# TensorE's instruction order laid out matmul by matmul in a fused attention and gated-MLP kernel

## The chip, the cores and the metric

The kernel runs on one core of one Trainium2 chip. Its time is in device microseconds (us) per execution. Engines are named PE (TensorE, matrix multiply), ACT (ScalarE), DVE (VectorE), POOL (GpSimd) and SP (SyncE, which here only starts DMA transfers). PE writes into PSUM; ACT and DVE read it out. Each engine works through its own queue in order, and an instruction waits for semaphores that others set.

## The reference

A layer normalisation of `x` (2048 x 640) feeds two branches. Branch A is attention in four segments of 512 rows with 32 heads of 20, causal inside a segment, joined by a memory of the earlier segments that is read through the feature map `phi`. Branch B is a gated MLP.

```python
xn = layernorm(x)
for s in range(4):                        # segments of 512 rows
    p = softmax(qs @ ks.T * scale + mask)
    a_dot = p @ vs
    a_mem = (phi(qs) @ M) / (phi(qs) @ z + 1e-6)
    o = g * a_mem + (1 - g) * a_dot       # g = sigmoid(beta), per head
    M, z = M + phi(ks).T @ vs, z + phi(ks).sum()
s = concat(o) @ wo                        # phi(t) = t + 1 if t > 0 else exp(t)
h = sigmoid(xn @ w_gate) * (xn @ w_up)
return x + s * silu(h @ w_down)
```

## The kernel before

Everything is bf16 with f32 sums. The order of all five engines is written out by hand: a Python planner calls functions that emit instructions, and the order of the calls is the order in each queue.

**Score batches and weighting passes.** A segment has 20 slots: four pairs of head groups, five units each (`UNITS`). In each slot `scores` (L471) emits one batch of 4 or 8 matmuls on four row strips of the array at once into the one PSUM tile `Sps`, ACT's exponential of 128 x 2048 (L482), and POOL's causal mask (L485). `weigh` (L489) multiplies the masked result by the values with 8 to 24 matmuls of 21 columns (L502) into the tile `Aps`, of which there is one; DVE then normalises it (L508 to L511).

**Dense groups.** A dense group is a chain of matmuls into one of three rotating PSUM buffers (`ps_d`), then an evacuation. `gate` (L386) and `up` (L394): five of 512 columns, then Tanh on ACT, or the product on DVE, which also needs gate's Tanh. `down` (L405): twelve of 320 columns, Tanh on ACT, product on DVE. `v_tile` (L313): five of 320, cast on ACT. `k_chunk`, `q_chunk` (L249, L274): five of 512, cast on DVE. `o_proj` (L450): five of 320, DVE. `m_update` (L343) and `mem_read` (L363) write and read the memory.

**The planner.** Gate, up and down groups wait in a list, `bulk`, with their cost in us. All else stands in a heap, `tasks`, with a due time in slots (`at`); the factor `R` is 20/24 slots, and `later` puts a step some of these units after the current time. Per slot the main loop (L628) emits `scores`, then fills 45% of the slot's budget, then emits the weighting passes of the slot before, then fills the other 55%. A fill runs the tasks that are due and whole bulk groups as long as half a group's cost is owed. So batches and passes always stand between groups. In the last segment three down groups are kept back for the end (`keep`).

**Features.** `phi` (L324) turns keys and queries into features: two DVE passes, Exp on ACT 0.5 units later, a maximum on DVE 0.5 units after that, and for keys a DMA transpose into `pkt` 0.7 units after that (L339), which `m_update` needs. The calls have fixed due times. The tile of keys (`k5`) has one buffer, so the next segment's keys wait for the transposes. Outgoing transfers of keys and queries (`stage_out`) read the same tiles that `phi` then overwrites.

**Startup.** Before the first slot: warm-up matmuls, normalisation of four row tiles (`ln_stats`: statistics on DVE, rstd on POOL; `ln_norm`: scaling on DVE L222, transposes on PE L229, copy on ACT), then all v, k, q groups of segment 0 and six gate and up groups.

Of the kernel before, what the change touches and what calls it, by code (L numbers as in the profile page):

```python
# [52 lines left out]
R = NSLOT / 24  # L53


@with_exitstack
def kernel(
# [37 lines left out]
    tasks = []  # L95
    count = [0]
    clock = [0.0]
# [5 lines left out]
    def later(lag, fn, *a):  # L103
        at(clock[0] + lag * R, 0.0, fn, *a)

# [143 lines left out]
    def k_chunk(n, c):  # L249
        s = st[n]  # L250
        if c == 0:
            s["k5"] = stg.tile([P, DC, L], BF, name="k5")
            s["kabs"] = stg.tile([P, DC], F32, name="kabs")
        ps = ps_d.tile([P, L], F32, name="psk", tag="d")
        for k in range(DC):
            nc.tensor.matmul(ps[:], lhsT=W["k"][:, k, c * P:(c + 1) * P], rhs=s["xnT"][:, k, :],  # L256
                             start=(k == 0), stop=(k == DC - 1))
        evacuate(n, s["k5"][:, c, :], ps[:])
        nc.vector.tensor_reduce(out=s["kabs"][:, c:c + 1], in_=s["k5"][:, c, :], axis=AX.X, op=ALU.max,  # L259
                                apply_absolute_value=True)  # L260
        if c in (2, 4) and n:
            later(0.9, stage_out, n, c // 4, Ks, KT, "k5")
        if c == DC - 1:
            s["IK"] = stg.tile([P, DC, H], BF, name="IK")
            nc.vector.tensor_tensor(s["IK"][:], nInd[:], s["kabs"][:].unsqueeze(2).to_broadcast([P, DC, H]),
                                    op=ALU.mult)

    def stage_out(n, half, src, dst, name):
        a, b = ((0, 3), (3, 5))[half]
        nc.sync.dma_start(src[n % 2][a * P:b * P, :].rearrange("(c p) n -> p c n", p=P), st[n][name][:, a:b, :])  # L270
        if n:
            later(1.0, relay, n, half, src, dst)

    def q_chunk(n, c):  # L274
        s = st[n]
        if c == 0:
            s["q5"] = stg.tile([P, DC, L], BF, name="q5")
            s["aq"] = stg.tile([P, DC, L], BF, name="aq")
        ps = ps_d.tile([P, L], F32, name="psq", tag="d")
        for k in range(DC):  # L280
            nc.tensor.matmul(ps[:], lhsT=W["q"][:, k, c * P:(c + 1) * P], rhs=s["xnT"][:, k, :],  # L281
                             start=(k == 0), stop=(k == DC - 1))
        evacuate(n, s["q5"][:, c, :], ps[:])
        nc.vector.tensor_scalar(s["aq"][:, c, :].bitcast(U16), s["q5"][:, c, :].bitcast(U16), 0x7FFF, None,
                                op0=ALU.bitwise_and)
        if c in (2, 4) and n:
            later(0.9, stage_out, n, c // 4, Qs, QT, "q5")

    def q_bound(n):
        s = st[n]  # L290
        ps = ps_d.tile([H, L], F32, name="cps", tag="d")
        for c in range(DC):
            nc.tensor.matmul(ps[:], lhsT=s["IK"][:, c, :], rhs=s["aq"][:, c, :],  # L293
                             start=(c == 0), stop=(c == DC - 1))
        cb = stg.tile([H, L], BF, name="cb")
        nc.scalar.copy(cb[:], ps[:])

        if n:
            later(0.8, c_out, n, cb)
        else:  # L300
            c_out(n, cb)

# [10 lines left out]
    def v_tile(n, j, half):  # L313
        s = st[n]
        ps = ps_d.tile([P, HB], F32, name="psv", tag="d")
        for k in range(DC):
            nc.tensor.matmul(ps[:], lhsT=s["xnT"][:, k, j * P:(j + 1) * P],  # L317
                             rhs=W["v"][:, k, half * HB:(half + 1) * HB],
                             start=(k == 0), stop=(k == DC - 1))
        va = V[4 * (n % 2) + j]  # L320
        nc.scalar.copy(va[:, half * 16:(half + 1) * 16, 0:DH], ps[:].rearrange("p (h e) -> p h e", e=DH))  # L321


    def phi(n, src, c):  # L324
        t = st[n][src][:, c, :]
# [8 lines left out]
        def rest():  # L334
            nc.vector.tensor_tensor(t, t, mn[:], op=ALU.max)
            if src == "k5":
                if c == 0:
                    st[n]["pkt"] = stg.tile([P, 4, D], BF, name="pkt")
                later(0.7, lambda: nc.sync.dma_start_transpose(st[n]["pkt"][:, :, c * P:(c + 1) * P], t))  # L339
        later(0.5, exp)  # L340


    def m_update(n, cs):  # L343
        s = st[n]
        dm = ps_d.tile([P, len(cs), HW * VW], F32, name="dm", tag="d")
        for i, c in enumerate(cs):
            w = (H1[c] - H0[c]) * VW
            for j in range(4):
                nc.tensor.matmul(dm[:, i, 0:w], lhsT=s["pkt"][:, j, c * P:(c + 1) * P],
                                 rhs=V[4 * (n % 2) + j][:, H0[c]:H1[c], :].rearrange("p h e -> p (h e)"),  # L350
                                 start=(j == 0), stop=(j == 3))
        for i, c in enumerate(cs):
# [10 lines left out]
    def mem_read(n, j, b):  # L363
        s = st[n]
        if j == 0 and b == 0:
            s["om"] = opool.tile([P, 4, D], BF, name="om", bufs=1)
        am = ps_d.tile([P, 16, VW], F32, name="am", tag="d")
        parts = [c for c in range(DC) if H0[c] < 16 * b + 16 and H1[c] > 16 * b]
        for i, c in enumerate(parts):
# [11 lines left out]
            am[:, :, 0:DH], rm[:].unsqueeze(2).to_broadcast([P, 16, DH]), op=ALU.mult)  # L381


    def gate(n, f):
# [3 lines left out]
        for k in range(DC):  # L388
            nc.tensor.matmul(gp[:], lhsT=Wg[f // 4][:, k, fo:fo + P], rhs=s["xnT"][:, k, :],  # L389
                             start=(k == 0), stop=(k == DC - 1))  # L390
        s["tg"] = gpool.tile([P, L], BF, name="tg")
        nc.scalar.activation(s["tg"][:], gp[:], ACT.Tanh, scale=0.5)  # L392

    def up(n, f):  # L394
# [3 lines left out]
        for k in range(DC):  # L398
            nc.tensor.matmul(ps[:], lhsT=Wu[f // 4][:, k, fo:fo + P], rhs=s["xnT"][:, k, :],  # L399
                             start=(k == 0), stop=(k == DC - 1))  # L400
        h = gpool.tile([P, L], BF, name="hT", bufs=FC)
        nc.vector.scalar_tensor_tensor(out=h[:], in0=s["tg"][:], scalar=1.0, in1=ps[:], op0=ALU.add, op1=ALU.mult)  # L402
        s.setdefault("hT", []).append(h)

    def down(n, j, half):  # L405
# [5 lines left out]
        for f in range(FC):  # L411
            nc.tensor.matmul(yp[:], lhsT=s["hT"][f][:, j * P:(j + 1) * P], rhs=W["d"][:, f, hs],  # L412
                             start=(f == 0), stop=(f == FC - 1))
        t2 = fpool.tile([P, HB], BF, name="t2")
        nc.scalar.activation(t2[:], yp[:], ACT.Tanh, scale=0.25)  # L415
        nc.vector.scalar_tensor_tensor(out=s[f"aa{j}"][:, hs], in0=t2[:], scalar=1.0, in1=yp[:],  # L416
                                       op0=ALU.add, op1=ALU.mult)

# [31 lines left out]
    def o_proj(n, j, half):  # L450
        s = st[n]
        aa, xr = s[f"aa{j}"], s[f"xr{j}"]
# [3 lines left out]
        for c in range(DC):  # L456
            nc.tensor.matmul(sp[:], lhsT=s["oT"][:, j, c, :], rhs=W["o"][:, c, hs],  # L457
                             start=(c == 0), stop=(c == DC - 1))
        nc.vector.scalar_tensor_tensor(out=aa[:, hs], in0=aa[:, hs], scalar=0.25, in1=sp[:],  # L459
# [4 lines left out]
        elif half == 1:  # L464
            (nc.gpsimd if n == NSEG - 1 else nc.vector).tensor_tensor(xr, aa[:], xr, op=ALU.add)
            later(0.9, lambda: nc.sync.dma_start(o2[rows, :], xr))

# [48 lines left out]
    bulk = [(1.09, fn, (0, f)) for f in range(FC) for fn in (gate, up)]  # L516

    def take(k):
        for _, fn, a in bulk[:k]:
            fn(*a)  # L520
# [7 lines left out]
    def startup():  # L528
# [5 lines left out]
        warm(10)  # L534
        ln_stats(0, 1, 0, 1)
        ln_norm(0, 0, 1)
        v_tile(0, 0, 0)
        ln_stats(0, 1, 1, 2)
        ln_norm(0, 1, 0)
        v_tile(0, 1, 0)  # L540
        ln_norm(0, 1, 1)
        v_tile(0, 2, 0)
        for j in range(3):
            v_tile(0, j, 1)
# [3 lines left out]
        for c in range(DC):  # L548
            k_chunk(0, c)
        nc.gpsimd.memset(KT[2][:], 1.0)  # L550
        stage_out(0, 0, Ks, KT, "k5")
        for c in range(DC):
            q_chunk(0, c)
# [7 lines left out]
        v_tile(0, 3, 0)  # L561
        v_tile(0, 3, 1)
        relay(0, 0, Qs, QT)
        q_bound(0)
# [18 lines left out]
    for n in range(NSEG):  # L583
        w = NSLOT * n
        m = n + 1
        if m < NSEG:
# [7 lines left out]
            for c in range(DC):  # L594
                at(w + R * (9.6 + 0.75 * c), 1.08, k_chunk, m, c)
                at(w + R * (13.4 + 0.75 * c), 1.08, q_chunk, m, c)
                at(w + R * (12.6 + 0.8 * c), 0.0, phi, m, "k5", c)
                at(w + R * (18.8 + 0.7 * c), 0.0, phi, m, "q5", c)
# [4 lines left out]
            if n == 0:  # L603
                for c in range(DC):
                    at(R * (2.6 + 0.8 * c), 0.0, phi, 0, "k5", c)
            for i, cs in enumerate(([0, 1, 2], [3, 4])):
                at(w + R * ((8.9 if n else 9.9) + i), 0.6, m_update, n, cs)
        if n >= 1:
# [3 lines left out]
            for i in range(8):  # L612
                at(w + R * (6.6 + i), 0.68, o_proj, n - 1, i // 2, i % 2)
                at(w + R * (3.0 + 0.75 * i), 0.35, mem_read, n, i // 2, i % 2)
# [5 lines left out]
    def run_task():  # L620
        time, _, cost, fn, a = heapq.heappop(tasks)
        clock[0] = max(clock[0], time)
        fn(*a)
        return cost

    owed = 0.0
    due, held = [], []
    for n in range(NSEG):  # L628
        st[n]["od"] = opool.tile([P, 4, D], BF, name="od")
        if n:  # L630
            bulk += [(1.09, fn, (n, f)) for f in range(FC) for fn in (gate, up)]
        bulk += [(1.64, down, (n, j, h)) for j in range(4) for h in range(2)]
        keep = 3 if n == NSEG - 1 else 0
        total = sum(b[0] for b in bulk[:len(bulk) - keep])
        total += sum(t[2] for t in tasks if t[0] < NSLOT * (n + 1))
        budget = total / NSLOT
        for slot in range(NSLOT):
            pair, u = divmod(slot, NU)
            now = NSLOT * n + slot

            def fill(until, share):
                nonlocal owed
                owed += budget * share
                while True:
                    if tasks and tasks[0][0] < until:
                        owed -= run_task()
                        if not (bulk and len(bulk) > keep and owed >= bulk[0][0] / 2):
                            continue
                    if bulk and len(bulk) > keep and owed >= bulk[0][0] / 2:
                        cost, fn, a = bulk.pop(0)  # L650
                        owed -= cost
                        fn(*a)
                    elif not (tasks and tasks[0][0] < until):
                        break

            pt = scores(n, pair, u)
            fill(now + 0.45, 0.45)
            for w in due:
                weigh(*w)
            due, held = held, []  # L660
# [3 lines left out]
            fill(now + 1.0, 0.55)  # L664
        while len(bulk) > keep:
            cost, fn, a = bulk.pop(0)
            owed -= cost
            fn(*a)


    for w in due:
        weigh(*w)
    while tasks:
        run_task()
    n = NSEG - 1
    for j in range(4):
        o_add(n, j, (DC - 1) * P, D)
    for i, (cost, fn, a) in enumerate(bulk):
        if i == len(bulk) - 1:
            o_last(n)  # L680
        fn(*a)
    for j in range(4):
        for h in range(2):
            o_proj(n, j, h)
            while tasks:
                run_task()
# [29 lines left out]
```

## Time and profile before

| | us |
|---|---|
| median of 3 runs | 349.03 (348.88 to 349.73) |
| the profiled execution, its own time | 350.11 |
| its span in the profile | 348.4 |
| PE's matmuls, start of the first score batch to the last matmul | 35.0 to 343.9 |
| segments 0, 1, 2 (first batch to first batch) | 72.8, 82.4, 82.4 |
| busy: PE, ACT, DVE, POOL | 330.7, 229.6, 227.6, 101.6 |

Times in the profile are from the start of the span. "L482" is line 482 of the kernel. In tables of waits a row reads: engine and line that waited, who ended the wait, total us, times, longest. In a timeline a row reads: start, length (of several merged instructions from first start to last end), engine, line, operation, tiles, count, and in brackets the engine's idle time before and who ended it. A matmul's length includes its way through the array, so starts, not lengths, tell the pace.

### The profile page before, as it was taken

To read this page: it belongs to the slowest core of one execution; us is meant where nothing else is said; L and a number is where in the kernel's file an instruction comes from. 1 tells how busy PE (TensorE), PEld (TensorE's weight loads), DVE (VectorE), ACT (ScalarE), POOL (GpSimd) and SP (SyncE) were. 2 spreads that over 40 slices of the span, in tenths; PEclk is the share of its full clock that TensorE was granted. 3 is DMA by queue.
4 is the path that set the end of the run, shared out by engine and by line. 5 is a ranking of instruction groups with operands and counts; after the bars stand their busy time and mean duration, and the time that the engine had idled before them with its cause. 6 is when DMAs were issued, how large, how long until landed. Compare 5 with 4: busy or idle time off the path is not lost.

```text
span 348.4 us, 8338 instructions
## 1 busy us (share of the span) xinstructions
PE 330.7 (95%) x3359; PEld 188.1 (54%) x3402; DVE 227.6 (65%) x581; ACT 229.6 (66%) x248; POOL 101.6 (29%) x135
## 2 busy tenths in 40 slices
PE   6999998997999999999999999999999999999995
PEld 5644445543665456654466446654456555545663
DVE  4252685499566576899655896699756478544355
ACT  2554869667796766557687676646778777767830
POOL 5930323232233233032222331312222232332314
PEclk9899999999999999999999999999999999999999
DMA  7964746565810851046840361123640140220032
GB/s 224 360 223 159 174 120 168 154 189 143 186 43 6 109 96 34 24 134 90 186 94 2 65 103 43 41 93 96 164 92 3 21 116 19 68 86 2 0 62 75
DMA packets 56581, 35.40 MB, mean 102 GB/s; under 512 B 31200, under 2 KB 56544, under 8 KB 56544
## 3 DMA queue, kind: packets, MB, share of 16 engines
q1 hardware_dynamic: 53024, 30.79, 36.2%
q10 hardware_dynamic: 3520, 4.10, 3.8%
q8 instruction: 26, 0.43, 0.5%
q14 instruction: 11, 0.09, 0.1%
HBM read 19.80 MB, written 8.00 MB: 80 GB/s over the span
## 4 chain that ended last, share of the span: by engine, by line
PE 69%; DVE 17%; issue 4%; ACT 4%; DMA 4%; POOL 1%; SPq 0%; DVEq 0%; ACTq 0%; POOLq 0%
PE yp L412 14%; PE up L399 12%; PE gp L389 12%; PE Aps L502 7%; PE Sps L477 6%; PE psq L281 5%; PE psv L317 5%; PE sp L457 5%; ACT pt L482 3%; DMA pkt<-k 2%; PE psk L256 2%; DVE k L247 2%; DVE kabs L259 2%; DVE hT L402 2%; PE cps L293 1%
## 5 line engine op out<-in xcount | busy, mean ns | idle before, releaser
L482 ACT ACTIVATE pt<-Sps 128x2048 bf16<-128x2048 f32 x80 | 150.1, 1876 | 33.2 <-PE Sps L477 32.0
L485 POOL TENSOR_SCALAR_AFFINE_SELECT pt<-pt 128x1024 bf16<-128x1024 bf16 (+1 forms) x80 | 75.9, 949 | 223.7 <-ACT pt L482 223.7
L399 PE MATMUL up<-xnT,Wu 128*128 128x512 bf16 x231 | 59.3, 379 | 1.0 <-DVE aa L459 0.5
L389 PE MATMUL gp<-xnT,Wg 128*128 128x512 bf16 x215 | 57.9, 379 | 1.5 <-issue 0.2
L412 PE MATMUL yp<-Wd,hT 128*128 128x320 bf16 x384 | 57.3, 299 | 0.0
L402 DVE SCALAR_TENSOR_TENSOR hT<-tg,up 128x512 bf16<-128x512 bf16 x48 | 32.8, 683 | 32.0 <-PE up L399 30.3
L502 PEld LDWEIGHTS <-pt 128*128 128x128 bf16 x1280 | 42.8, 96 | 14.3 <-issue 2.3
L502 PE MATMUL Aps<-va,pt 128*128 128x21 bf16 x1280 | 44.6, 173 | 1.1 <-POOL pt L485 0.7
L412 PEld LDWEIGHTS <-hT 128*128 128x128 bf16 x384 | 35.1, 97 | 15.3 <-issue 3.0
L392 ACT ACTIVATE tg<-gp 128x512 bf16<-128x512 f32 x48 | 28.5, 593 | 17.4 <-PE gp L389 17.4
L416 DVE SCALAR_TENSOR_TENSOR aa<-t,yp 128x320 bf16<-128x320 bf16 x32 | 15.6, 487 | 33.5 <-ACT t L415 33.3
L477 PE MATMUL Sps<-QT,KT 21*128 21x128 bf16 (+3 forms) x512 | 31.7, 300 | 4.4 <-ACT pt L482 4.3
L399 PEld LDWEIGHTS <-Wu 128*128 128x128 bf16 x240 | 20.9, 97 | 23.7 <-issue 3.4
L389 PEld LDWEIGHTS <-Wg 128*128 128x128 bf16 x240 | 20.3, 97 | 22.2 <-issue 4.1
L331 ACT ACTIVATE mn<-mn 128x512 bf16<-128x512 bf16 x35 | 22.1, 631 | 13.2 <-DVE mn L327 13.2
L317 PE MATMUL psv<-Wv,xnT 128*128 128x320 bf16 x160 | 27.7, 309 | 0.3 <-DVE hT L402 0.3
L457 PE MATMUL sp<-Wo,oT 128*128 128x320 bf16 x160 | 25.8, 299 | 0.0
L415 ACT ACTIVATE t<-yp 128x320 bf16<-128x320 f32 x32 | 14.0, 437 | 17.1 <-PE yp L412 17.1
L477 PEld LDWEIGHTS <-KT 21*128 21x128 bf16 x512 | 9.5, 92 | 28.7 <-issue 27.4
L256 PE MATMUL psk<-xnT,Wk 128*128 128x512 bf16 x94 | 23.9, 379 | 0.7 <-DVE k L247 0.3
L281 PE MATMUL psq<-xnT,Wq 128*128 128x512 bf16 x97 | 23.8, 380 | 0.5 <-DVE hT L402 0.4
L321 ACT CAST va<-psv 128x320 bf16<-128x320 f32 x32 | 13.7, 431 | 14.6 <-PE psv L317 14.1
(74 smaller groups left out, 330.4 us busy)
## 6 DMA issues: line engine op xcount, KB each, us to landing
KT<-Ks SPq DMA_DIRECT2D x32, 80.0 KB
QT<-Qs SPq DMA_DIRECT2D x32, 80.0 KB
xr<-in_A_x_dram SPq DMA_DIRECT2D x15, 160.0 KB
out_dram<-xr SPq DMA_DIRECT2D x15, 160.0 KB
xt<-in_A_x_dram SPq DMA_DIRECT2D x6, 320.0 KB
Wd<-in_B_w_down_dram ACTq DMA_DIRECT2D x1, 1920.0 KB
Ks<-k SPq DMA_DIRECT2D x4, 384.0 KB
Qs<-q SPq DMA_DIRECT2D x4, 384.0 KB
```

The costliest lines, as they stand in the source:

```text
L256: nc.tensor.matmul(ps[:], lhsT=W["k"][:, k, c * P:(c + 1) * P], rhs=s["xnT"][:, k, :], start=(k == 0), stop=(k == DC - 1))
L281: nc.tensor.matmul(ps[:], lhsT=W["q"][:, k, c * P:(c + 1) * P], rhs=s["xnT"][:, k, :], start=(k == 0), stop=(k == DC - 1))
L317: nc.tensor.matmul(ps[:], lhsT=s["xnT"][:, k, j * P:(j + 1) * P], rhs=W["v"][:, k, half * HB:(half + 1) * HB], start=(k == 0), stop=(k == ...
L389: nc.tensor.matmul(gp[:], lhsT=Wg[f // 4][:, k, fo:fo + P], rhs=s["xnT"][:, k, :], start=(k == 0), stop=(k == DC - 1))
L399: nc.tensor.matmul(ps[:], lhsT=Wu[f // 4][:, k, fo:fo + P], rhs=s["xnT"][:, k, :], start=(k == 0), stop=(k == DC - 1))
L402: nc.vector.scalar_tensor_tensor(out=h[:], in0=s["tg"][:], scalar=1.0, in1=ps[:], op0=ALU.add, op1=ALU.mult)
L412: nc.tensor.matmul(yp[:], lhsT=s["hT"][f][:, j * P:(j + 1) * P], rhs=W["d"][:, f, hs], start=(f == 0), stop=(f == FC - 1))
L457: nc.tensor.matmul(sp[:], lhsT=s["oT"][:, j, c, :], rhs=W["o"][:, c, hs], start=(c == 0), stop=(c == DC - 1))
L477: nc.tensor.matmul(Sps[:, r, c0:c0 + ncol], lhsT=kt[32 * r:32 * r + VW, gi, kb * P:(kb + 1) * P], rhs=qt[32 * r:32 * r + VW, gi, kb * P:L] ...
L482: nc.scalar.activation(pt[:], Sps[:], ACT.Exp, scale=SCALE)
L485: nc.gpsimd.affine_select(out=diag, in_=diag, compare_op=ALU.is_ge, fill=0.0, base=0, pattern=[[0, 4], [0, cnt], [1, P]], channel_multipli ...
L502: nc.tensor.matmul(A[:, qb, r, :], lhsT=pt[:, r, off:off + P], rhs=V[4 * (n % 2) + kb][:, 4 * g + r, :], start=first, stop=True, skip_grou ...
```

## The change

Each function that emits matmuls becomes a generator which hands control back after every matmul with its cost (0.216 us for 512 columns, 0.136 for 320). The planner keeps one unit open (`cur`), takes the next from tasks that are due (`ready`) and otherwise from `bulk`, and moves its position `pos` by cost over budget; weighting passes count as well. Batches and passes are emitted when `pos` reaches the slot's begin and its middle, also inside an open group.

```diff
+    def step(keep):
+        if cur[0] is None:
+            if ready:
+                cur[0] = ready.pop(0)
+            elif len(bulk) > keep:
+                _, fn, a = bulk.pop(0)
+                cur[0] = fn(*a)
+            else:
+                return None
+        cost = next(cur[0], None)
...
+    def advance(target, budget, keep):
...
+            if pos[0] >= target:
+                return
+            cost = step(keep)
+            if cost is None:
+                pos[0] = min(target, tasks[0][0]) if tasks else target
+            else:
+                pos[0] += cost / budget
...
@@ gate; k_chunk, q_chunk, q_bound, v_tile, up, down, o_proj alike
             nc.tensor.matmul(gp[:], lhsT=Wg[f // 4][:, k, fo:fo + P], rhs=s["xnT"][:, k, :],
                              start=(k == 0), stop=(k == DC - 1))
+            if k < DC - 1:
+                yield T512
         s["tg"] = gpool.tile([P, L], BF, name="tg")
         nc.scalar.activation(s["tg"][:], gp[:], ACT.Tanh, scale=0.5)
+        yield T512
...
@@ the main loop
             pt = scores(n, pair, u)
-            fill(now + 0.45, 0.45)
+            advance(now + 0.5, budget, keep)
             for w in due:
                 weigh(*w)
+                pos[0] += weigh_cost(w[2], w[3]) / budget
...
-            fill(now + 1.0, 0.55)
+            advance(now + 1.0, budget, keep)
```

Features go through a queue: at most two are under way, a new one starts at the earliest 0.75 units after the last, and they are pushed when the outgoing transfer has been emitted.

```diff
+    def phi_go():
+        if phis and live[0] < 2 and not held_back[0]:
+            live[0] += 1
+            held_back[0] = True
+            later(0.75, phi_next)
+            phi(*phis.pop(0))
...
@@ phi
-        later(0.5, exp)
+        later(0.8, exp)
@@ stage_out
+            for c in range(a, b):
+                later(1.9 if name == "q5" else 0.7, phi_push, n, name, c)
```

Due times, kept groups, startup and end:

```diff
-                at(w + R * ((8.9 if n else 9.9) + i), 0.6, m_update, n, cs)
+                at(w + R * (10.0 + i), 0.7, m_update, n, cs)
...
-                at(w + R * (3.0 + 0.75 * i), 0.35, mem_read, n, i // 2, i % 2)
+                at(w + R * (4.0 + 0.75 * i), 0.2, mem_read, n, i // 2, i % 2)
...
-        keep = 3 if n == NSEG - 1 else 0
+        keep = 4 if n >= NSEG - 2 else 0
...
         warm(10)
+        ln_norm(0, 0, 1)
         ln_stats(0, 1, 0, 1)
-        ln_norm(0, 0, 1)
...
+    take(1)
     for w in due:
         weigh(*w)
```

The four groups that segment 2 keeps back are down groups; they are the first of segment 3's list. At the end one of the last four down groups comes ahead of the last weighting pass, two behind it, then the last transposes of the attention output (`o_last`), then the fourth. Every matmul, activation and transfer of the old program is in the new one, once.

## The prediction, made before the changed kernel ran

> **What bounds the kernel now.** I read the page first, then the waits, the chain of waits, and the timeline around each wait of the tensor engine (PE).
>
> ```profile
> PE 330.7 (95%) x3359; PEld 188.1 (54%) x3402; DVE 227.6 (65%) x581; ACT 229.6 (66%) x248; POOL 101.6 (29%) x135
> ```
>
> PE is busy for 95% of the span, so only its order, its waits and the two ends can give time. What its work weighs is in the chain of waits, whose pieces are start, length, what:
>
> ```profile
> 29.69 1.08 PE up L399 x5
> ...
> 58.07 7.70 DMA pkt<-k
> ...
> 92.33 1.64 PE yp L412 x12
> ```
>
> One 512-column matmul takes 1.08/5 = 0.216 us, one 320-column matmul 1.64/12 = 0.136. In the same way a weighting matmul (L502) takes 0.025, a memory matmul 0.065, and a score batch 0.41: 0.32 from its first matmul to the next dense one, and about 0.09 more that its first start comes late. From the first batch at 35.02 to the end of the last matmul at 343.85 the program has 615 x 0.216 + 664 x 0.136 + 132 x 0.065 + 1280 x 0.025 + 80 x 0.41 = 296.8 us of work (and 0.2 of transposes). 308.8 passed, so 12.0 us is all that a better order can win there. By segment the loss is 5.9, 1.6, 1.6 and 2.9 us. Going from start to start, I find 9.9 us of it in nineteen gaps of 0.14 to 1.26 us. The waits view (us, times, longest) names who ended the largest:
>
> ```profile
> PE Sps L477 <- ACT pt L482: 4.3, 6, 1.2
> ...
> PE am L371 <- DVE om L379: 0.8, 2, 0.4
> PE Aps L502 <- POOL pt L485: 0.7, 1, 0.7
> ```
>
> The first row is the score batch: one PSUM tile `Sps`, which the exponential (L482) must have read before the next batch may write it. A typical case:
>
> ```profile
> 79.36 1.86 ACT L482 ACTIVATE pt<-Sps 128x2048 bf16<-128x2048 f32 x1
> ...
> 80.07 0.56 PE L502 MATMUL Aps<-va,pt 128*128 128x21 bf16 x16
> ...
> 81.27 0.40 PE L477 MATMUL Sps<-QT,KT 21*128 21x512 bf16 x4 [0.64 <-ACT pt L482]
> ...
> 81.59 1.25 PE L281 MATMUL psq<-xnT,Wq 128*128 128x512 bf16 x5
> ```
>
> The slot before it held one dense group and 16 weighting matmuls, 1.9 us of work; the exponential alone takes 1.86. In start-to-start gaps the seven such waits cost 0.97, 0.68, 1.26, 0.67, 0.38, 0.14 and 0.72 = 4.8 us. They stand after slots with 1.7 to 2.3 us of work, but for the 1.26, where a feature exponential ran ahead on ACT.
>
> **The change, part by part.**
>
> *Even slots.* The new order has the same matmuls. Priced by the same rows, its slots hold 3.3 to 3.5 us of work in segment 0 (before: 1.9 to 4.5), 3.9 to 4.3 in segment 1, 3.6 to 3.9 in segment 2 and 2.9 to 3.2 in segment 3; four down groups of segment 2 go into segment 3, where slots went down to 1.7. An exponential starts 0.5 us after its batch and takes 1.88, so 2.4 us suffice while less than 0.6 to 1.0 us of other ACT work stands ahead of it. I added up ACT's work between exponentials in the new order: in segment 0 it goes up to 4.2 us in one slot, but what spills over, at most 0.8, fits. One batch stays late, by 0.3. Term: -4.8 + 0.3 = -4.5 (bounds -4.8 and -3.0).
>
> *What a cut group does to ACT.* Before, every batch stood between groups, so the evacuation of the group before it was in ACT's queue ahead of the exponential:
>
> ```profile
> 210.00 0.39 PE L477 MATMUL Sps<-QT,KT 21*128 21x512 bf16 x4
> ...
> 210.11 0.43 ACT L321 CAST va<-psv 128x320 bf16<-128x320 f32 x1 [1.58 <-PE psv L317]
> ...
> 210.51 1.88 ACT L482 ACTIVATE pt<-Sps 128x2048 bf16<-128x2048 f32 x1
> ```
>
> Now 64 of the 80 batches cut a group open, 19 of them a gate or a v group. That group's Tanh or cast is issued after the exponential and waits it out, and the third group from there needs its buffer (`ps_d` has three). The worst place, slot 7 of segment 2: the batch cuts a v group after two of five matmuls; then come 3 x 0.136, a memory read 0.2 and a projection group 0.68, so the third group is due 0.32 + 0.41 + 0.20 + 0.68 = 1.6 us after the batch began; its buffer is free after 0.5 + 1.88 + 0.32 (the cast, which overlaps the exponential's end by 0.1) + 0.06 = 2.76. PE waits 1.1 us; DVE's chain behind it does not wait longer. Going through all batches this way, twelve places come out late: 0.46, 0.54, 0.18 in segment 0; 0.80, 0.81, 0.67 in segment 1; 0.18, 0.06, 0.35, 0.14, 1.07 in segment 2; 0.40 and 0.21 (one exponential, I count 0.40) in segment 3: 5.7 us. The same reading of the old order gives 0.2. At three of them PE stood already for DVE beside memory reads (gaps of 0.54, 0.55, 0.69 before), and PE waits once where two things are late; I take 1.5 off: +4.2 (bounds +1.5, if most overlap, and +9.1, if all 19 pay the mean of 0.48).
>
> *The switch itself.* A batch begins 0.10 later than the stream would and the next matmul 0.09 later, 80 times in the old order. The Trainium skill, "TensorEngine Tiling (Array Packing)", Key Properties, says that a change of tiling mode drains TensorE. Read as a warning, it speaks against cutting groups: 64 further drains of 0.19 would be 12 us. But each batch leaves and re-enters the dense stream once in both orders, so I add nothing; the rows cannot show a cut group, so up to 0.05 a batch stays in the range (3 us). A weighting pass amid dense matmuls costs 0.02 at its edges before, and nothing more is added.
>
> *Features.* The Min, Exp and Max passes are as many as before; the queue only spaces them, in ACT and DVE time that the sums above hold. Their steps come 2.0 instead of 1.7 units after each other, so the last `pkt` transpose of segment 0 is issued about 0.25 slot, 0.9 us, nearer to the 1.9 MB load of `Wd`, which stretched the transfer to the 7.70 us in the chain. DVE's cast of `k` waited 2.0 us for it and PE lost 0.5 behind that; everything in DVE's queue waits too, hT and the release of `Aps` first. Term +0.3 (0 to +1.5). Later m_update and mem_read: 0; what needs them is four units on. SP's other issues keep their order but for one or two places.
>
> *Startup.* The second normalisation (L222) moves ahead of the statistics of the next tile:
>
> ```profile
> 5.30:8.70 3.40, 1.67 (x26) 1.33 (x25) 2.15 (x7) 0.69 (x1) 1.48 (x4) 1.00 1.00 303
> 8.70:12.10 3.40, 3.40 (x22) 2.22 (x19) 1.88 (x5) 1.81 (x3) 2.77 (x11) 0.51 1.08 378
> ```
>
> ```profile
> 6.92 0.49 DVE L211 BATCH_NORM_STATS2 bs<-xt 128x6 f32<-128x320 bf16 x1 [1.22 <-DMA xt<-in_A_x_dram]
> ...
> 7.97 0.39 DVE L222 TENSOR_SCALAR xn<-xt,mv,rstd 128x640 bf16<-128x640 bf16 x1
> ...
> 8.42 0.46 PE L229 MATMUL pT<-ident,xn 128*128 128x128 bf16 x5 [1.65 <-DVE xn L222]
> ```
>
> (The first two: stretch, its length, busy PE, PEld, DVE, ACT, POOL, then granted clock, DMA share, GB/s.) Its rstd is ready at 6.40, so it fits DVE's idle 1.22 us: transposes at 6.9 and the first v group at 7.3 instead of 8.7. What is late next is the second pair: x lands at 6.92, statistics and rstd end at 9.1, so the fourth tile's v group starts near 12.0 at the half clock of the second stretch, or near 11.1 at the full clock, instead of 12.46. Term -0.9 (bounds -0.5, -1.4). The Trainium skill, "TensorE: Matmul & The Clock Gate", Part 1, says that an idle window of some 3.4 us halves the clock; the 0.51 after a stretch with 1.67 us of work agrees, and if 2.3 us of work there kept the clock, the term would be the larger.
>
> *The end.* A down group now stands ahead of the last weighting pass, which waited 0.69 for POOL (0.83 start to start). Behind the last exponential a Tanh then comes late for the third down group, by about 0.5. Term -0.3 (-0.8 to 0).
>
> Sum: -4.5 + 4.2 + 0.3 - 0.9 - 0.3 = -1.2 us. The profiled execution took 350.11 (span 348.4 and 1.7 around it), so 348.9; the median shown is 1.08 lower, so 347.8.
>
> **The rivals.**
> (a) *The buffer waits mostly overlap* with DVE's old ones, and the clock stays up at the start: -4.8 + 1.5 + 0 - 1.4 - 0.5 = -5.2, 343.8. For it: waits of one place are paid once. Against it: the worst places (0.80, 0.81, 1.07) are above what the old gaps there held.
> (b) *The waits change places only:* +5.7 for the twelve, the rest as above: -4.5 + 5.7 + 0.3 - 0.9 - 0.3 = +0.3, 349.3.
> (c) *Slower: evacuation behind the exponential becomes PE's bound.* If all 19 cut gate and v groups pay the mean 0.48: +9.1 instead of +4.2, so +3.7, 352.7. It decides from 6.5 us of such waits on. For it: `ps_d` has three buffers and ACT has 59.8 us of work in segment 0 against 66.9 of PE's; against it: by the reading above the rest of the 19 come out in time.
> (d) *The evenness does not hold,* as work planned in matmul costs leaves waits out: -1.5 instead of -4.5, all else as forecast, +1.8, 350.8. The planned shares are too even for it to be likely.
>
> **How the numbers follow.** About 0.3%, 1.05 us, is what a measurement tells from no change. My forecast, 346 to 348.5, gets 0.36; (a) 0.17; (b) 0.20; (c) 0.20; (d) 0.07. Faster: 0.17 and most of the forecast's 0.36, 0.49; same: 0.23; slower: 0.28. The forecast is 347.8 by the sum. The range runs from (a), 343.8, to short of (c), 351.8, which leaves out about a fifth; the forecast's own is 346 to 348.5.
>
> **What would show it.** After: the row `Sps <- ACT pt` under 1 us; new PE waits of v, gate, projection and memory groups on ACT's casts and Tanh, 3 to 6 us together; the first v group at 7.3; the first batch near 34.1 instead of 35.0; segments 1 and 2 losing more than 1.6 us each to waits, segment 0 under 3. It is wrong if dense matmuls after a batch start more than 0.10 late throughout, if buffer waits stay under 1.5 us or pass 6.5, or if the last `pkt` transfer holds DVE for over 3 us.

## The result, and the profile after

The changed kernel takes 354.75 us (median of 4 runs, 354.05 to 355.14) beside 349.12 for the kernel before: 1.0156 times as long, 95% interval [1.0135, 1.0178]. The change made the kernel slower, by 5.6 us where 1.2 us of gain was forecast, and the time lies above the range. The profiled execution took 354.9, its span is 353.2.

The page's busy times, in the same row as before:

```profile
PE 334.6 (95%) x3402; PEld 186.6 (53%) x3402; DVE 231.4 (66%) x581; ACT 230.5 (65%) x248; POOL 101.2 (29%) x135
```

The shares have not moved, so this row tells nothing. (The profile before lacks 43 of the 3402 matmul records, so its PE time is a little low.) The waits of PE do tell something (who waited, who ended it, total us, times, longest):

```profile
PE gp L474 <- DVE om L463: 1.4, 2, 1.0
...
PE psq L327 <- DVE aa L557: 1.3, 2, 0.8
PE cps L342 <- DVE aq L332: 1.1, 1, 1.1
PE cps L342 <- DVE hT L492: 0.9, 1, 0.9
PE Sps L576 <- DMA QT<-Cs: 0.8, 1, 0.8
PE gp L474 <- ACT va L375: 0.7, 1, 0.7
PE psv L369 <- DVE hT L492: 0.7, 1, 0.7
...
PE psv L369 <- ACT tg L479: 0.4, 1, 0.4
PE Sps L576 <- ACT pt L581: 0.3, 1, 0.3
```

The row at the head of the list before, 4.3 us of score batches waiting for the exponential, is at 0.3: the change does what it says. In its place stand many rows of dense groups (`gp`, `psq`, `cps`, `psv`), and most end on DVE. Counted from start to start in gaps of 0.12 us and more, as in the prediction, waits from the first batch on were 9.9 us and are 14.2. Exponential before a batch: 4.8, now 0.4. Buffers that Tanh or the value cast empties: 0.2, now 3.1. Ended by POOL: 0.8, now none. Ended by DVE: 3.7, now 10.5 (`om` 3.4, `aa` 2.5, `hT` 2.1, `aq` 1.5, others 1.0).

| from first batch to first batch, us | before | after |
|---|---|---|
| up to the first batch | 35.0 | 35.0 |
| segment 0 | 72.8 | 71.6 |
| segment 1 | 82.4 | 85.4 |
| segment 2, with the four down groups (6.5 us) that now go to segment 3 | 82.4 | 79.7 + 6.5 |
| segment 3, without them, to the last matmul's end | 71.4 | 77.2 - 6.5 |

Segments 0 and 3 gain 1.2 and 0.7, segments 1 and 2 lose 3.0 and 3.8. The two profiled executions thus differ by 4.9 us from the first batch on; this way of counting is called "by segments" below. A cut group in segment 0, in the timeline of the changed kernel:

```profile
60.83 0.40 PE L576 MATMUL Sps<-QT,KT 21*128 21x256 bf16 x8
...
61.16 0.39 PE L474 MATMUL gp<-xnT,Wg 128*128 128x512 bf16 x1
...
61.34 1.88 ACT L581 ACTIVATE pt<-Sps 128x2048 bf16<-128x2048 f32 x1 [1.07 <-PE Sps L576]
61.38 1.39 PE L369 MATMUL psv<-Wv,xnT 128*128 128x320 bf16 x9
...
63.11 0.59 ACT L479 ACTIVATE tg<-gp 128x512 bf16<-128x512 f32 x1
...
63.75 0.43 PE L369 MATMUL psv<-Wv,xnT 128*128 128x320 bf16 x2 [0.44 <-ACT tg L479]
```

The batch comes one matmul before the end of a gate group. ACT starts the exponential at 61.34, so the Tanh, whose input was complete at 61.55 (the last matmul's start and length), starts at 63.11, and the third group behind the gate group waits for its buffer. That is the step the prediction called "a cut group". The second kind is at the query bound, whose last query group now stands right ahead of it:

```profile
88.06 1.04 PE L342 MATMUL cps<-aq,IK 128*32 128x512 bf16 x4
...
88.56 0.67 DVE L400 TENSOR_SCALAR mn<-k 128x512 bf16<-128x512 bf16 x1
...
89.26 0.29 DVE L401 TENSOR_SCALAR k<-k 128x512 bf16<-128x512 bf16 x1
...
89.47 0.68 DVE L287 CAST q<-psq 128x512 bf16<-128x512 f32 x1
...
90.18 0.29 DVE L332 TENSOR_SCALAR aq<-q 128x512 uint16<-128x512 uint16 x1
...
90.53 0.38 PE L342 MATMUL cps<-aq,IK 128*32 128x512 bf16 x1 [1.11 <-DVE aq L332]
```

The fifth matmul of `cps` needs the fifth query chunk, which DVE casts at 89.47, behind feature passes of the keys. The third kind is a DVE that is simply behind. Windows of the kernel before (stretch, length, busy PE, PEld, DVE, ACT, POOL, granted clock as a share of full speed, DMA share, GB/s):

```profile
82.00:89.00 7.00, 5.75 (x39) 2.38 (x38) 6.76 (x18) 5.04 (x5) 1.13 (x2) 1.00 0.65 182
152.00:159.00 7.00, 6.75 (x62) 3.39 (x62) 6.79 (x16) 3.83 (x6) 1.78 (x2) 1.00 0.26 84
239.00:246.00 7.00, 6.89 (x61) 3.12 (x62) 6.79 (x18) 4.78 (x6) 1.37 (x2) 1.00 0.46 109
```

and of the changed one:

```profile
82.00:89.00 7.00, 7.00 (x74) 3.71 (x73) 6.76 (x18) 5.12 (x5) 1.96 (x3) 1.00 0.97 215
152.00:159.00 7.00, 6.17 (x67) 3.38 (x66) 6.72 (x15) 2.67 (x2) 1.78 (x2) 1.00 0.52 164
246.00:253.00 7.00, 5.69 (x59) 2.47 (x57) 6.72 (x17) 4.37 (x6) 1.90 (x2) 1.00 0.47 132
```

Where keys and queries are made (in segment 2 up to 4 us later in the changed kernel), DVE is busy for 6.7 to 6.8 of 7 us in both kernels. In the old order PE loses little there in segments 1 and 2 (6.75, 6.89 busy); in the new one it waits for DVE (6.17, 5.69).

It is tempting to say that the old order's pauses for the exponential, such as the one between 82 and 89 (5.75 busy), let DVE keep up, and that PE pays at DVE once they are gone. The trace does not bear this out for the segments that lose: the old order's seven late batches start at 56.12, 81.27, 86.41, 103.41, 284.22, 286.65 and 302.38, so all are in segments 0 and 3, and none is in segments 1 and 2 (107.8 to 272.6). What does differ there is the order of the groups. From 145 to 160 the old order has an `up` group (150.4) and a `gate` group (156.1) among those of keys, queries, projections and memory; in the new one no group of `bulk` starts there, because a unit that is due goes ahead of `bulk`. In segment 2 it is the same from 225 to 245. One of the waits that follow, for a projection that DVE has not yet emptied:

```profile
158.67 0.81 PE L327 MATMUL psq<-xnT,Wq 128*128 128x512 bf16 x3 [0.83 <-DVE aa L557]
```

No run spreads these groups out with all else the same, so that their order is the reason is a reading of the trace, not a result.

### The profile page after: what moved, and what is told of

Same layout as the page of the kernel before. It is cut to its first block, busy times and chain, and to the rows that moved or that the text cites. A ratio compares the mean times of both kernels' runs of the same rounds, so it can differ in the third digit from the quotient of the medians.

```text
span 353.2 us, 8387 instructions
## 1 busy us (share of the span) xinstructions
PE 334.6 (95%) x3402; PEld 186.6 (53%) x3402; DVE 231.4 (66%) x581; ACT 230.5 (65%) x248; POOL 101.2 (29%) x135
## 4 chain that ended last, share of the span: by engine, by line
PE 67%; DVE 18%; issue 5%; DMA 5%; ACT 3%; POOL 1%; SPq 1%; ACTq 0%; DVEq 0%
PE yp L503 14%; PE up L487 13%; PE gp L474 12%; PE Aps L601 7%; PE Sps L576 6%; PE psv L369 4%; PE sp L553 4%; PE psk L296 3%; PE psq L327 3%; DVE aa L557 2%; DVE k L287 2%; DVE kabs L301 2%; DMA Ks<-k 2%; ACT pt L581 1%; DVE xr L563 1%
## 5 line engine op out<-in xcount | busy, mean ns | idle before, releaser
L474 PE MATMUL gp<-xnT,Wg 128*128 128x512 bf16 x240 | 64.4, 379 | 2.8 <-DVE om L463 1.4
L487 PE MATMUL up<-xnT,Wu 128*128 128x512 bf16 x240 | 64.8, 379 | 0.7 <-DVE om L463 0.7
L503 PE MATMUL yp<-Wd,hT 128*128 128x320 bf16 x384 | 58.8, 299 | 0.0
L601 PEld LDWEIGHTS <-pt 128*128 128x128 bf16 x1280 | 43.7, 96 | 16.0 <-issue 1.9
L474 PEld LDWEIGHTS <-Wg 128*128 128x128 bf16 x240 | 21.2, 97 | 26.3 <-issue 6.4
L553 PE MATMUL sp<-Wo,oT 128*128 128x320 bf16 x160 | 27.1, 299 | 1.1 <-DVE rm L460 0.6
L327 PE MATMUL psq<-xnT,Wq 128*128 128x512 bf16 x100 | 24.9, 379 | 1.3 <-DVE aa L557 1.3
L296 PE MATMUL psk<-xnT,Wk 128*128 128x512 bf16 x100 | 25.0, 379 | 0.1
L557 DVE SCALAR_TENSOR_TENSOR aa<-aa,sp 128x320 bf16<-128x320 bf16 x32 | 15.5, 483 | 7.0 <-PE sp L553 6.8
L553 PEld LDWEIGHTS <-oT 128*128 128x128 bf16 x160 | 14.5, 97 | 9.6 <-issue 2.9
```

The costliest lines, as they stand in the source:

```text
L601: nc.tensor.matmul(A[:, qb, r, :], lhsT=pt[:, r, off:off + P], rhs=V[4 * (n % 2) + kb][:, 4 * g + r, :], start=first, stop=True, skip_grou ...
```

## The experiments

Each starts from the changed kernel unless another is named. Times are medians; ratios are to the kernel before, run beside them.

**What cutting costs.** Nothing is cut (e1), and score batches leave only gate and value groups whole (e4):

```diff
# e1
-            if pos[0] >= target:
+            if pos[0] >= target and cur[0] is None:
                 return
# e4
-            if pos[0] >= target:
+            if pos[0] >= target and not (cur[0] is not None and cur[0].__name__ in whole):
                 return
...
-            advance(now + 1.0, budget, keep)
+            advance(now + 1.0, budget, keep, ("gate", "v_tile"))
```

> The new planner, but a batch or a pass waits until the open group is finished, so nothing cuts a group. Theory A (evacuations issued behind the exponential, on ACT and through hT on DVE's queue): the waits for buffers that ACT empties (3.1 us in the changed kernel) and for hT (2.1 us) nearly go, and with them some of DVE's lateness: 350 to 351.5 us. Theory B (DVE's long busy stretch, made worse by taking four down groups out of segment 2): within 1 us of 354.75. Theory C (due tasks run back to back, so that small groups rotate three buffers too fast): within 1 us of 354.75.

> The changed kernel, but score batches do not cut gate and v groups (19 places); all else is cut as before. Theory A in its narrow form (the evacuation of the very group that is cut): the 3.1 us for ACT's buffers fall under 1 and hT's go, 350.5 to 352. If the lateness is DVE's own: 353.5 to 355.

e1: 351.67, ratio 1.0064 [1.0039, 1.0090]. e4: 350.39, 1.0029 [1.0010, 1.0048]. Both lie within 0.2 us of the times that theory A gave. By the medians, leaving only the groups that ACT evacuates whole gives 4.4 us back, and leaving all whole 3.1. By segments both give the same 3.6 (first batch to the last matmul: 313.9 in the changed kernel, 310.3 in e1 and in e4), so that one is better than the other is not shown. The 4.4 holds some startup as well: the first batch of e4's profiled execution is 0.6 earlier, which its edit does not touch.

The waits (start to start) fall by as much, from 14.2 to 10.6 in e4, but not quite where it was expected. Those for buffers that ACT empties go from 3.1 to 2.0, not under 1: 0.9 of the rest stands behind two whole value groups that follow a batch (the `va` row above), and is there in e1 too, where nothing is cut. More comes back by way of DVE: `om` from 3.4 to 1.4 and `hT` from 2.1 to 1.2, while `aq` grows from 1.5 to 2.3.

**The division of the 4.4** (e11: `whole` is `("gate",)` alone).

> The changed kernel with score batches that leave only the gate groups whole; value groups are still cut. It divides the 4.4 us that leaving both whole brought. By the trace of the changed kernel, waits for buffers that Tanh empties are 1.7 us, and waits for hT (Tanh late, VectorE's queue held) 2.1, against 1.4 for buffers that the value cast empties: expected 351.3 to 352.0 (2.8 to 3.4 of the 4.4 belong to the gate). If it is the value cast that matters, 353 or more; if the gate groups carry all of it, 350.4.

354.24, 1.0127 [1.0098, 1.0156]: outside what was expected, and where the value cast was said to matter. In the profiled execution (354.26) part of it is the startup, where the clock was at 0.65 in a stretch in which the changed kernel had 1.00; its first batch is at 35.71. By segments, which leave this out, whole gate groups bring 1.4 us and whole value groups a further 2.2 (e11: 70.9, 85.4, 79.6, 76.6; e4: 70.9, 84.7, 78.1, 76.6). The value groups' part does not come from waits that end on their casts, for of these 0.9 in e11 and 1.2 in e4 are left: with the value groups whole, waits of 0.56 and 0.81 for `om` go, and one of 1.1 for `hT`.

**Carried groups, feature queue, memory steps** (e2, e3, e8):

```diff
# e2
-        keep = 4 if n >= NSEG - 2 else 0
+        keep = 4 if n == NSEG - 1 else 0
# e3: no queue; features at fixed due times as before
+                at(w + R * (13.6 + 0.8 * c), 0.0, phi, m, "k5", c)
+                at(w + R * (19.2 + 0.7 * c), 0.0, phi, m, "q5", c)
# e8
-                at(w + R * (10.0 + i), 0.7, m_update, n, cs)
+                at(w + R * ((8.9 if n else 9.9) + i), 0.7, m_update, n, cs)
-                at(w + R * (4.0 + 0.75 * i), 0.2, mem_read, n, i // 2, i % 2)
+                at(w + R * (3.0 + 0.75 * i), 0.2, mem_read, n, i // 2, i % 2)
```

> The changed kernel with four groups kept back in the last segment alone, so segment 2 has its eight down groups again. Theory B: segment 2 loses 1.6 us to waits instead of 5.4 (79.7 us for 74.3 of work), segment 3 gets its short slots back (+1 to +2): 352 to 353. Theories A and C: the sum moves by under 1 us.

> The changed kernel without the queue of features: fixed due times (0.8 and 0.7 units apart, as late as the outgoing transfer demands), Exp 0.5 units after the first passes. If the queue puts features where DVE has no room, the waits for aq, q and aa in the key and query stretch (about 4 us in three segments) halve: 352 to 353. Otherwise within 1 us of 354.75.

> The changed kernel with memory reads one unit earlier and memory updates 1.1 units earlier, due as in the kernel before (cost entries left as changed). If these due times bring the waits for om, rm and aa (6.1 us in the changed kernel): 352 to 353. If what matters is that small groups follow each other within DVE's three steps: 354 to 356.

e2: 355.26, 1.0168 [1.0150, 1.0185]. e3: 356.34, 1.0207 [1.0179, 1.0236]. e8: 355.41, 1.0168 [1.0142, 1.0194]. None of the three is a cause. The feature queue is worth some 1.6 us to the new order, more than was expected of it. So neither the cuts (e1 still loses 1.3 us in segment 1 and 3.5 in segment 2) nor the carried groups nor these due times alone explain what segments 1 and 2 lose.

**The query bound's place** (e5; e6 is e4 and e5 together):

```diff
-                at(w + R * (17.2), 1.12, q_bound, m)
+                at(w + R * (18.6), 1.12, q_bound, m)
```

> The changed kernel with q_bound due 1.4 units later, so that one or two down groups stand between the last query group and it. In the changed kernel PE waits 1.2 us in segment 0 and 1.4 us in segment 2 at q_bound, for DVE's aq of the query group just before it and for a buffer that hT holds. Theory D (a task that is due is taken at once, ahead of bulk, and so stands right behind the group whose DVE result it reads): about 2.5 us less, 352.2. Rival (DVE is late in that stretch whatever stands there): the wait moves to the down groups' buffers or the next query groups, within 1 us of 354.75.

> No cuts of gate and v groups by score batches, and q_bound 1.4 units later. Theory A and D together: 350.4 less some 3 us (the trace of the kernel without those cuts shows 3.4 us of waits at q_bound), 347 to 348, under the kernel before. Rival as above: 350.

e5: 352.71, 1.0097 [1.0074, 1.0121], so 2.0 us. e6: 348.0, 0.9958 [0.9942, 0.9974]: the two parts add up (4.4 + 2.4; by segments 3.6 + 2.5), and the kernel is 0.4% faster than before. What goes is the wait for `aq`; the 0.9 us for `hT` in segment 2 only moves to the `up` group that now stands there, as the rival had it.

**The startup** (e7 and e10 start from the kernel before, e9 from e6):

```diff
# e7, e10
+        ln_norm(0, 0, 1)
         ln_stats(0, 1, 0, 1)
-        ln_norm(0, 0, 1)
# e9, e10
-    for i in range(2):
-        load_glu(i, 0)
-        load_glu(i, 1)
+    load_glu(0, 0)
+    load_glu(0, 1)
...
         c_in(0, (0,))
+        load_glu(1, 0)
         x_load(1, 0)
+        load_glu(1, 1)
         x_load(1, 1)
```

> The kernel before with the second normalisation moved up, and nothing else. The prediction: 0.9 us less, 348.3 (bounds 0.5 and 1.4). Rival (the first score batch waits for the transfer of the bound into the query tile, which does not come earlier because the transfers before it share the queues with the weights): first v group at 7.3, but first batch at 34.7 or later, and the time within 0.4 us of 349.2.

> The kernel with gate and value groups left whole and the query bound later, with one thing more: the loads of the second column blocks of the gate and up weights (2 x 640 KB) leave the head of the SP queue and are issued behind the first part of the query bound's relay. Theory S (the 0.9 us that the startup gained on TensorE are held back by the transfers to the query tile, whose first write stands behind all weight loads): the first query relay is issued by 27.3, the first score batch starts by 34.2 without a wait for the query tile, and the time goes from 348.0 to 347.3 or 347.7. Rival (the ScalarE pace or the later groups' waits take it back): the first batch starts by 34.2, but the time stays within 0.3 of 348.0. Worse if the blocks land after the fourth gate group wants them at about 38 us: then a wait for Wg shows and the time is 348.5 or more.

> The kernel before with two edits of the startup alone: the second normalization moved up, and the second column blocks of the gate and up weights loaded behind the first part of the query bound's relay. Theory S: the first batch starts 0.8 to 1.1 us earlier than before (33.9 to 34.2) and the time is 348.3 to 348.7, where the first edit alone gave 349.42. Rival: the first batch is earlier, but the slots of the first segment give it back (the score batches of that segment wait for the exponential), and the time stays at 349.2 to 349.6.

e7: 349.42 beside 349.46, 1.0002 [0.9986, 1.0018]. e9: 348.2, 0.9969 [0.9956, 0.9982], no better than e6. e10: 349.86, 1.0010 [0.9995, 1.0025]. The first batch is where it was expected with the later loads (34.08 and 34.17, no wait for the query tile), but e6, without them, has it at 34.16 in its profile, so e9 shows no effect of them. In e10 segment 0 is 1.35 us longer: a value group waits 1.6 us for the next segment's transposed rows (`xnT`). The rows now load behind 640 KB of weights, but so they do in e9, which has no such wait; e10 tells little. e7's interval is -0.5 to +0.6 us, which leaves out the forecast 0.9.

**The late DVE** (e12 from e6, e13 from the changed kernel, e14 from the kernel before):

```diff
-    def evacuate(n, dst, ps):
-        if n == 0:
+    def evacuate(n, dst, ps, c=0):
+        if n == 0 or c % 2:
             nc.scalar.copy(dst, ps)
...
-        evacuate(n, s["q5"][:, c, :], ps[:])
+        evacuate(n, s["q5"][:, c, :], ps[:], c)
```

(the same in `k_chunk`)

> The kernel with gate and value groups left whole and the query bound later, with one thing more: in segments 1 to 3 the odd key and query chunks (4 of 10 in each) are evacuated by ScalarE and not by VectorE. Theory V (what is left of the waits ends on a VectorE that is late in the stretches where keys and queries are made: 6.72 to 6.76 us busy of each 7 between 145 and 166 and between 225 and 246, with ScalarE at 2.9 to 5.2): 4 x 0.69 us leave VectorE in each of these stretches, waits for aa, om and hT behind 150 us shrink from 5.0 to under 2.5, and the time is 345.0 to 347.0. Rival (ScalarE's exponential then becomes the late one): the waits for aa and hT shrink, but score batches wait for the exponential, or the chunks' own buffers come free late behind it, for as much, and the time is 347.7 to 349.

> The changed kernel, its cut groups and its query bound's due time left as they are, with the odd key and query chunks of segments 1 to 3 evacuated by ScalarE. It prices the late VectorE by itself. Theory V (VectorE late in the key and query stretches is the part of the loss that was left out): the waits for aq behind the query bound, for hT at the query bound and for aa go (4.5 us in the trace of the changed kernel at 88 to 91, 158, 229, 237 to 253), and the time falls from 354.75 to between 350.0 and 352.0. Rival (ScalarE is already late in the cut groups, so more work on it lengthens the waits that Tanh and the value casts end): those waits grow from 3.1 us to over 5, and the time stays at 353 or more.

> The kernel before with the same one edit. If the lateness of VectorE in the key and query stretches was there before the change at the same price, the time falls by as much as from the kernel with whole groups (2.6 us), to 346.2 to 347.2; if the change's order made it, by less than 1, since only about 1 us of the waits of the kernel before fall in these stretches (aa 0.5, hT 0.4): 348.2 to 349.2; above 349.5 if ScalarE's work delays the exponentials that the score batches of before already wait for (4.8 us).

e12: 345.4 (345.12 to 346.58), 0.9895 [0.9865, 0.9924]. That is 2.6 us below e6 (2.2 by the ratios, 2.7 by segments). The waits behind 150 us fall from 5.1 to 2.5, and the windows of e12 read:

```profile
152.00:159.00 7.00, 7.00 (x73) 3.44 (x71) 5.88 (x13) 4.79 (x6) 2.20 (x2) 1.00 0.43 127
239.00:246.00 7.00, 7.00 (x70) 3.25 (x69) 6.69 (x18) 5.47 (x9) 1.87 (x2) 1.00 0.47 131
```

and those of e6, from which it starts:

```profile
152.00:159.00 7.00, 6.17 (x66) 3.17 (x65) 6.75 (x15) 3.33 (x4) 2.25 (x2) 1.00 0.36 113
239.00:246.00 7.00, 5.83 (x60) 2.73 (x59) 6.72 (x17) 5.02 (x6) 1.92 (x2) 1.00 0.51 149
```

PE is busy throughout where e6 had it at 6.17 and 5.83. e13: 351.56, 1.0053 [1.0035, 1.0070], 3.2 us below the changed kernel. e14: 351.19, 1.0039 [1.0021, 1.0056], 1.4 above its kernel before. The same edit helps the new order and hurts the old one, so the new order made DVE late at a price that the old one did not pay. The row `Sps <- ACT pt` falls from 4.3 to 3.3 in e14, where the expectation saw the exponentials delayed, but its query bounds now wait for a Tanh (the row for `QT` is of the startup, which the edit does not touch):

```profile
PE Sps L477 <- ACT pt L482: 3.3, 5, 0.9
...
PE Sps L477 <- DMA QT<-Cs: 1.9, 1, 1.9
...
PE cps L293 <- ACT tg L392: 1.3, 3, 0.6
```

e12 beats both kernels: it is 9.4 us below the changed one and, by the ratio above, about 1% below the one before. Against the kernel before, by segments and with the four down groups counted where they were, e12 gains 3.9 in segment 0 and 1.3 in segment 3, the two in which the old order's batches were late, and loses 1.2 and 0.1 in segments 1 and 2.

## Why the prediction was wrong

*Even slots, -4.5:* right. Start to start, 4.8 became 0.4, and e12 gains in the segments where those waits were; no run evens the slots alone. (The prices printed for the work add up to 296.5 us, not 296.8; nothing behind it changes by that.)

*What a cut group does to ACT, +4.2:* near in size (4.4 by e4's median, 3.6 by segments), and that is partly luck. The rival that put 9.1 there is out, and so is the one in which the waits only overlap. But the term was added up from waits for buffers that ACT empties, and whole groups take only 1.1 of these away; the larger part goes by way of DVE, of whose chain the prediction said that it "does not wait longer". At the place that it called the worst, PE waits 0.81 where 1.07 was forecast, and for DVE (`rm`, at 220.89). How the cuts delay DVE is not shown in full. Its waits for `tg` went from 1.6 to 8.1 us:

```profile
DVE hT L402 <- ACT tg L392: 1.6, 2, 1.4
DVE hT L492 <- ACT tg L479: 8.1, 5, 2.5
```

With the gate groups whole (e11) these are gone, but that brings back 1.4 us by segments, not 3.6.

*The switch, 0:* right. In cut groups the batch begins 0.10 late and the next matmul 0.09 late, as between groups before. The warning that was weighed there put 12 us on it, and no run shows any of that.

*Features, +0.3:* wrong in sign. Nothing waits for `pkt` any more, where DVE waited 2.0 before, and without the queue the new order takes 1.6 us more (e3).

*Startup, -0.9:* failed. The first v group came at 7.3, as forecast, and the clock was at 1.00 between 8.70 and 12.10. But the term was read against a profiled execution with half clock in that stretch, and taken off a median of runs that need not have had it. e14 has the startup of before, unchanged, at full clock; its windows:

```profile
5.30:8.70 3.40, 2.14 (x27) 1.53 (x25) 2.86 (x9) 1.24 (x2) 1.88 (x4) 1.00 0.99 323
8.70:12.10 3.40, 2.65 (x25) 1.80 (x25) 1.16 (x2) 2.60 (x6) 3.14 (x10) 1.00 1.08 366
```

In e14 PE is through with the work ahead of the first batch at 33.77, in the changed kernel at 34.11: with the clock at 1.00 from 8.70 to 12.10 in both, the moved normalisation brings PE nothing (one execution each). What then ends the stage differs from execution to execution. In e14 the batch waits 1.86 for the query tile (`QT<-Cs`) and starts at 35.63, in the changed kernel 0.84 (34.95). In the twelve profiles with the moved normalisation and the loads in their old places it starts at 34.0 to 34.3 in eight, as forecast, and at 34.8 to 35.7 in four. The timed runs of e7 show no gain.

*The end, -0.3:* the wait for POOL is gone, and segment 3 gained 0.7 in all; what of it is the tail was not taken apart.

*What the sum left out* is the step that failed. Waits that end on DVE were taken as they were before: the prediction followed only ACT's queue behind a cut group, held that DVE's chain does not wait longer, put later memory steps at 0, and had no term for DVE behind the new order of groups. They went from 3.7 to 10.5 us. Of its own signs, "segment 0 under 3" failed too: the segments lose 4.6, 4.6 and 5.4 us to waits. Two terms were missing. The query bound directly behind the last query group, which was not in the sum at all: +2.0 (e5), or +2.4 (e4 to e6). A DVE that is late in the key and query stretches of the new order: +2.6 (e6 to e12), or 3.2 taken alone (e13, where it overlaps with the query bound's waits). By the medians the account reads -4.4 + 4.4 + 2.0 + 2.6 = +4.6 of the 5.6 measured; by segments it is -4.4 + 3.6 + 2.5 + 2.7 = +4.4 of 4.9. So 1.0 or 0.5 is left open, and so is why DVE is late in the new order, as said above.

## What to carry to other kernels

A new order can make an engine late whose work has not changed. Before the price of a removed wait is counted as gain, list which other engines are near full in each stretch (here DVE at 97%) and follow their queues in the new order too, also in stretches where no wait is removed. Filling at the grain of a matmul cost nothing on PE here, but a batch that cuts a group puts a long activation ahead of that group's evacuation: leaving whole the groups that ACT empties was worth 3.6 us by segments, and cutting the others was neither gain nor loss (e1 beside e4). And a term that is read from one profiled execution may be taken off that execution's time alone, not off a median of others.

## What the runs showed of the hardware

The clock in the startup differs from execution to execution of one instruction order. In the kernel before, a stretch (5.30 to 8.70) with 1.67 us of matmuls in 3.40 was followed by a clock of 0.51; in e14, with the same startup, one with 2.14 was followed by 1.00. In e11, which has the changed kernel's startup, the same stretch also held 2.14, and the clock was 0.85 in the next and 0.65 from 12.10 on. So the work in such a stretch does not decide it alone here, and none of these stretches was idle, as the prediction's reading of the 0.51 would need. The Trainium skill, "TensorE: Matmul & The Clock Gate", Part 1, says that the activity window runs free, so that the same kernel can fall on either side; these executions agree. It is a spread that no edit here made: the first v group is at 8.71 or 7.95 in the old startup, and the first batch, where it does not wait for the query tile, at 34.0 to 34.2 or 35.71 in the new one.
